# A product of ones behind the spreading product, and the cap of both w_out placed behind GpSimd's addition for block 1

## The chip, the core and the metric

The kernel runs on one core of a Trainium2 chip. The metric is the device time of one execution in microseconds (us); five executions of the kernel before gave a median of 307.3 us (306.88, 307.03, 307.30, 309.13 and 309.36). The core has TensorE (PE; PEld is its weight load), VectorE (DVE), ScalarE (ACT), GpSimd (POOL) and SyncE (SP), which here only issues transfers. Each engine takes its instructions in the order in which the program gives them.

## What is computed

A polynomial attention without a softmax, and behind it a gated feed-forward layer:

```python
# q, k, v: (4, 4, 1088, 32); S1, S2: (8, 32); w_gate, w_val: (128, 1536); w_out: (1536, 128)
a = einsum('rd,bhsd->bhsr', S1, x); b = einsum('rd,bhsd->bhsr', S2, x)      # phi(x): 8 x 8 = 64 features
q_p, k_p = phi(q), phi(k)
kv  = einsum('bhsf,bhsd->bhfd', k_p, v);  z = sum(k_p, axis=2)
x   = einsum('bhsf,bhfd->bhsd', q_p, kv) / (einsum('bhsf,bhf->bhs', q_p, z) + 1e-6)
x   = x.transpose(0, 2, 1, 3).reshape(4352, 128)
out = (1 / (1 + exp(-(x @ w_gate))) * (x @ w_val)) @ w_out
```

S1, S2 and the three weights arrive as 64-bit floats, seen as pairs of 32-bit words, and are narrowed to 32 bits inside the kernel.

## The kernel before, in words

**Tiling.** The feed-forward layer is cut into chunks of 512 tokens (`tok_chk`) and twelve blocks `j` of 128 hidden units. `w1` issues one "wave": the gate and value products of one block for one chunk into the two banks of a PSUM tile `wave` (pool `psm`, two buffers), then ScalarE's sigmoid; its `glu` is VectorE's product of the two. `w2` adds block `j` into the chunk's output sum (`moeout`). `slot(group, waves)` places a piece of attention work and then that many waves. A float32 product appears in the profile as two MATMUL instructions, so a wave is four (512 columns each), and a `w2` step two.

**The start.** The attention of batch 0 must give the first 512 columns of `xT`, the layer's input, before any wave can run. On TensorE the order is: products of ones (`warm`, L255 to L261, whose result nothing reads), the turning of S, `kps` (keys times S), `ab` (queries times S, L542), `gram` with its 36 small products (L468), two further `ab`, the spreading product `spread_z` (L497), the denominators `dps` (L730), the key-value sums `kvz` in two groups of 40 and 32 instructions (L638, called from `rest`), the transposition `ndps` (L708), the numerators `nps` (L749), one more `warm(256)` (L868), and then the waves (L363). Between these VectorE makes the outer products `kp` (L530), the mask `zm` and `zb` behind the spreading product (L508, L520), the transposition `dT` of the denominators (L741), and in `divide` (L757) a reciprocal and two halves of `xT` (L776), each behind a transposition `rb` (L765). ScalarE copies between: `kvd` (L674) and `nd` (L721).

**The narrowing.** `narrow` (L83) works in four steps, with a `yield` between them: step 0 is GpSimd's `cap` (L97) and ScalarE's `tail` (L101), which both read what the transfer brought; step 1 is VectorE's two instructions on `head` (L105, L109); step 2 is ScalarE's `square` (L117) and GpSimd's addition into `head` (L118); step 3 is VectorE's product into `w_sb` (L127). For blocks 0 and 1 `narrow_01(part, step)` (L187) takes three parts: part 0 is gate and value of block 0, part 1 gate and value of block 1, part 2 both w_out. For the other blocks it is `narrow_w(j, step)`, three weights of one block at a time. Steps 0 of all three parts stand ahead of `spread_z()` (L844). Steps 1 and 2 of part 0 stand in `rest` (L863), which `dn` runs between denominators and numerators. In `divide` the function `head1` (L870) is run between the first `rb` and the first half of `xT`; it has part 1's step 1, part 0's step 3, part 1's step 2, and step 0 of blocks 2 and 3. Part 1's step 3 and part 2's steps 1 and 2 follow behind `divide`; part 2's step 3 comes in the second wave (L374).

**Transfers.** All loads of the first batch are issued by SyncE (the keys by ScalarE) at the very start, in the order of L239 to L249. Nothing of them depends on the lines that the change touches.

Of the kernel before, what the change touches and what calls it, by code (L numbers as in the profile page):

```python
# [20 lines left out]
def kernel(  # L21
# [61 lines left out]
    def narrow(out, bits, eng, bank=None, copies=None):  # L83

        p, n, m = bits.shape[:3]
        lo, hi = bits[:, :, :, 0].bitcast(U32), bits[:, :, :, 1]

        def tmp(dt, tag, bufs):
            return sbN.tile([P, 3, P], dt, tag=tag, name=tag, bufs=bufs)[:p, :n, :m]

        cap, tail = tmp(I32, "cap", 6), tmp(I32, "tail", 5)
        eng.tensor_scalar(  # L97
            out=cap.bitcast(F32), in0=hi.bitcast(F32), scalar1=122880.0, scalar2=-122880.0,
            op0=ALU.min, op1=ALU.max,
        )  # L100
        nc.scalar.activation(out=tail, in_=lo, func=ACTF.Copy, scale=2.0**-29)  # L101
        yield

        head = tmp(I32, "head", 3)
        nc.vector.tensor_scalar(  # L105
            out=head, in0=cap, scalar1=3, scalar2=0x3FFFFFF8,
            op0=ALU.logical_shift_left, op1=ALU.bitwise_and,
        )
        nc.vector.scalar_tensor_tensor(  # L109
            out=head, in0=cap, scalar=-0x40000000, in1=head, op0=ALU.bitwise_and, op1=ALU.bitwise_or  # L110
        )
        yield
        square = cap.bitcast(F32)
        if bank:
            square = pso.tile([P, 512], F32, tag=bank, name="square")[:, : n * m]
            square = square.rearrange("p (n m) -> p n m", n=n)
        nc.scalar.activation(out=square, in_=cap.bitcast(F32), func=ACTF.Square)  # L117
        nc.gpsimd.tensor_tensor(out=head, in0=head, in1=tail, op=ALU.add)  # L118
        yield

        head = head.bitcast(F32)
        if copies:
            square, head = (
                bass.AP(tensor=x.tensor, offset=x.offset, ap=[list(x.ap[0]), [0, copies], [1, m]])
                for x in (square, head)
            )
        nc.vector.scalar_tensor_tensor(  # L127
            out=out, in0=square, scalar=1.265625 * 2.0**-30, in1=head, op0=ALU.is_ge, op1=MUL
        )
        yield  # L130
# [44 lines left out]
    def narrow_w(j, step):  # L175
        if not 0 <= j < NJ:
            return
        n, jj = divmod(j, 2)
        if wide:
            if step == 0:  # L180
                narrowing[j] = narrow(
                    w_sb[:, :, j, :], w_in[n][:, :, jj], nc.gpsimd, "acc1" if j < NJ - 2 else None
                )
            next(narrowing[j])


    def narrow_01(part, step):  # L187
        if wide:
            if step == 0:
                i = (slice(0, 2), part) if part < 2 else (2, slice(0, 2))  # L190
                narrowing["01", part] = narrow(
                    w_sb[:, i[0], i[1]],
                    w_in[0][:, i[0], i[1]],
                    nc.gpsimd,
                    "acc0" if part else "acc1",
                )
            next(narrowing["01", part])
# [57 lines left out]
    def warm(*cols):  # L255
        t = psm.tile([P, 2, 512], F32, tag="wave", name="warm")
        one = [bass.AP(tensor=ones.tensor, offset=ones.offset, ap=[list(ones.ap[0]), [0, n]]) for n in cols]
        x = bass.AP(tensor=ones.tensor, offset=ones.offset, ap=[list(ones.ap[0]), [0, P]])
        for r in one:
            n = r.shape[-1]  # L260
            nc.tensor.matmul(out=t[:, 0, :n], lhsT=x, rhs=r, start=True, stop=True)  # L261
# [265 lines left out]
    def outer(b, pi, j0=0, j1=NJK):  # L527
        a0 = KAB[b][:, pi, j0:j1]
        ap = [list(a0.ap[0]), [2 * R, 2 * (j1 - j0)]]
        nc.vector.tensor_tensor(  # L530
            out=KP[b][:, pi, j0:j1].rearrange("p j m (i l) -> p (j m) i l", i=R),
            in0=bass.AP(tensor=a0.tensor, offset=a0.offset, ap=ap + [[1, R], [0, R]]),
            in1=bass.AP(tensor=a0.tensor, offset=a0.offset + R, ap=ap + [[0, R], [1, R]]),
            op=MUL,
        )
# [6 lines left out]
    def ab(a_of=None, b_of=None, pool_b=None):  # L542

        mm = []
        if a_of is not None:
            aps = psm.tile([P, 2, 512], F32, tag="wave", name="aps")
            mm.append((a_of, aps, sa))
        if b_of is not None:
            pool, tag = (ps2, "two") if pool_b is None else pool_b
            bps = pool.tile([P, 2, 512], F32, tag=tag, name="bps")  # L550
            mm.append((b_of, bps, sb))
        for c in range(2):
            for m in range(2):
                for (bb, pr, n), dst, sx in mm:
                    h = 2 * pr + m
                    rows = slice(32 * h, 32 * h + 32)
                    t0, tn = q_chk[n]
                    nc.tensor.matmul(
                        out=dst[64 * c : 64 * c + 64, m, : 32 * tn],
                        lhsT=sx[rows, :],  # L560
                        rhs=qT_of[bb][rows, t0 : t0 + tn, c, :],
                        start=True,
                        stop=True,
                    )
        if a_of is not None:
            w = 32 * q_chk[a_of[2]][1]
            ASB[a_of] = sbA.tile([P, 2, 256], F32, tag="asb", name="asb", bufs=2)
            nc.scalar.copy(out=ASB[a_of][:, :, :w], in_=aps[:, :, :w])
        if b_of is not None:

            def mult():
                bb, pr, n = b_of
                if bb not in QP:
                    QP[bb] = sbA.tile([P, 2 * H * W1], F32, tag="qp", name="qp")
                t0, tn = q_chk[n]
                w = 32 * tn
                nc.vector.tensor_tensor(  # L577
                    out=half(QP[bb], n).rearrange("p (m c) w -> p c m w", m=2)[:, pr],
                    in0=bps[:, :, :w],
                    in1=ASB[b_of][:, :, :w],  # L580
                    op=MUL,
                )

            return mult
# [256 lines left out]
    spread_z, mask_z = gram()  # L841
    mult00 = ab(None, (0, 0, 0))
    mult10 = ab(None, (0, 1, 0), (psm, "wave"))
    for part in range(3):  # L844
        narrow_01(part, 0)
    spread_z()
    for pi in range(2):
        outer(0, pi, 0, 5)
    mult00()
# [20 lines left out]
    def head1():  # L870
        narrow_01(1, 1)
        narrow_01(0, 3)
        narrow_01(1, 2)
        narrow_w(2, 0)
        narrow_w(3, 0)

    divide((0, 4), (4, 8), between=head1)
    narrow_01(1, 3)
    narrow_01(2, 1)
# [86 lines left out]
```

## Time and profile before

The profiled execution took 307.03 us, of which 305.0 us lie between its first and last instruction (the span); 2.0 us lie around it.

| engine | busy us | share of the span | instructions |
|---|---|---|---|
| TensorE | 297.5 | 98% | 1364 |
| TensorE weight load | 138.3 | 45% | 1364 |
| VectorE | 155.3 | 51% | 267 |
| ScalarE | 80.7 | 26% | 150 |
| GpSimd | 35.4 | 12% | 63 |

Busy time is summed from the first to the last instruction of each engine's records; TensorE's products are pipelined, so that a busy TensorE need not be one at its peak. The profile also tells the share of full speed that TensorE's clock was granted (PEclk). In the chain of work that ended last, TensorE has 96% of the span, 58% of it in the waves and 30% in `moeout`. In a listing by time, a bracket such as `[1.18 <-DVE zb L520]` says how long the engine had been idle before the row and what ended that.

### The profile page before, as it was taken

How to read it: one execution, taken by the hardware profiler on the slowest of the kernel's cores; microseconds unless marked ns; L12 is line 12 of the kernel's file. 1: busy time of each engine (PE TensorE's matmuls, PEld its weight loads, DVE VectorE, ACT ScalarE, POOL GpSimd, SP SyncE). 2: the span in 40 equal slices, each digit the busy share in tenths (PEclk: the TensorE clock that was granted, in tenths of full speed). 3: DMA queues.
4: the chain of work that ended last, by engine and by line, in shares of the span. 5: the costliest groups of instructions: out<-in, count | busy, mean ns of one | idle time of the engine just before them, and what ended most of it. 6: DMA issues, size and time to landing. Idle time of an engine off the chain costs nothing.

```text
span 305.0 us, 3608 instructions
## 1 busy us (share of the span) xinstructions
PE 297.5 (98%) x1364; PEld 138.3 (45%) x1364; DVE 155.3 (51%) x267; ACT 80.7 (26%) x150; POOL 35.4 (12%) x63
## 2 busy tenths in 40 slices
PE   8799999999999999999999999999999999999994
PEld 3454434444344444443444444444444444444683
DVE  7887888865546544564365543645232223222331
ACT  3455542221123222212222222221222222222220
POOL 1545560410000500000004100000000000000000
PEclk9789999999999999999999999999999999999999
DMA  7992531597102594440004910200010000200011
GB/s 230 335 335 62 126 116 42 133 225 190 65 0 37 120 160 69 78 157 27 0 8 125 212 39 2 36 0 2 0 20 15 0 0 5 31 0 0 8 27 17
DMA packets 29585, 23.29 MB, mean 76 GB/s; under 512 B 20928, under 2 KB 24512, under 8 KB 29568
## 3 DMA queue, kind: packets, MB, share of 16 engines
q1 hardware_dynamic: 25200, 15.21, 18.5%
q0 software_dynamic: 3456, 7.09, 11.9%
q10 hardware_dynamic: 912, 0.77, 0.9%
q8 instruction: 10, 0.16, 0.2%
q14 instruction: 7, 0.06, 0.1%
HBM read 19.80 MB, written 3.26 MB: 76 GB/s over the span
## 4 chain that ended last, share of the span: by engine, by line
PE 96%; DVE 1%; DMA 1%; issue 0%; ACT 0%; SPq 0%; DVEq 0%
PE wave L363 58%; PE moeout L320 30%; PE nps L749 2%; PE dps L730 2%; PE kvz L652 1%; PE kps L451 1%; PE kvz L638 1%; DMA s_in<-in_S_dram 1%; PE cqps L597 1%; PE warm L261 0%; PE ndps L708 0%; DVE kT L428 0%; PE gram L474 0%; PE kvz L661 0%; DVE qp L577 0%
## 5 line engine op out<-in xcount | busy, mean ns | idle before, releaser
L363 PE MATMUL wave<-xT,w_sb 128*128 128x512 f32 (+1 forms) x436 | 192.0, 566 | 0.0
L384 DVE TENSOR_TENSOR g<-wave,sg 128x512 f32<-128x512 f32 x102 | 70.4, 690 | 132.8 <-ACT sg L371 132.5
L363 PEld LDWEIGHTS wave<-xT,w_sb 128*128 128x128 f32 x436 | 83.3, 191 | 93.1 <-issue 88.7
L371 ACT ACTIVATE sg<-wave 128x512 f32<-128x512 f32 x102 | 60.9, 597 | 201.9 <-PE wave L363 201.9
L320 PE MATMUL moeout<-g,w_sb 128*128 128x512 f32 (+1 forms) x216 | 105.4, 576 | 0.0
L320 PEld LDWEIGHTS moeout<-g,w_sb 128*128 128x128 f32 x216 | 39.5, 190 | 43.6 <-issue 38.2
L621 POOL DMA_DIRECT2D qp<-dq x12 | 7.0, 587 | 109.5 <-DMA dq<-cq 109.5
L118 POOL TENSOR_TENSOR head<-head,tail 128x384 int32<-128x384 int32 (+2 forms) x14 | 13.6, 971 | 17.9 <-DVE head L109 14.3
L530 DVE TENSOR_TENSOR kp<-kab 128x1152 f32<-128x1152 f32 (+2 forms) x10 | 10.8, 1096 | 0.0
L630 DVE TENSOR_TENSOR qp<-qp,bq 128x1152 f32<-128x1152 f32 (+1 forms) x7 | 9.1, 1294 | 0.3 <-DMA bq<-dq 0.2
L109 DVE SCALAR_TENSOR_TENSOR head<-cap,head 128x384 int32<-128x384 int32 (+2 forms) x14 | 7.5, 535 | 0.5
L330 DVE STREAM_TRANSPOSE o_sb<-moeout 128x512 f32<-128x512 f32 (+1 forms) x9 | 6.1, 680 | 2.6 <-PE moeout L320 2.5
L97 POOL TENSOR_SCALAR cap<-w_in 128x384 f32<-128x384 f32 (+1 forms) x13 | 7.0, 543 | 1.3 <-DMA w_in<-in_moe_w_out_dram 1.3
L101 ACT ACTIVATE tail<-w_in 128x384 int32<-128x384 uint32 (+1 forms) x13 | 6.6, 524 | 2.0 <-DMA w_in<-in_moe_w_out_dram 2.0
L621 POOL DMA_DIRECT2D bq<-dq x12 | 6.9, 576 | 0.5 <-DMA out_dram<-o_sb 0.2
L776 DVE TENSOR_TENSOR xT<-nps,rb 128x576 f32<-128x576 f32 (+2 forms) x9 | 5.9, 661 | 1.9 <-PE nps L749 1.3
L127 DVE SCALAR_TENSOR_TENSOR w_sb<-square,head 128x384 f32<-128x384 f32 (+1 forms) x11 | 5.6, 519 | 1.9 <-POOL head L118 1.6
L730 PE MATMUL dps<-qp,zb 128*32 128x256 f32 (+1 forms) x64 | 5.4, 409 | 1.2 <-DVE zb L520 1.2
L261 PE MATMUL warm<-ones 128*128 128x512 f32 (+2 forms) x10 | 5.5, 682 | 1.0 <-DVE hm L267 1.0
L749 PE MATMUL nps<-qp,nd 64*32 64x256 f32 (+1 forms) x128 | 6.0, 432 | 0.4 <-ACT nd L721 0.4
L765 DVE STREAM_TRANSPOSE rb<-rc 128x576 f32<-128x576 f32 (+2 forms) x9 | 6.1, 680 | 0.3
L439 DVE STREAM_TRANSPOSE qT<-kq 128x512 f32<-128x512 f32 (+1 forms) x8 | 5.7, 715 | 0.0
(73 smaller groups left out, 85.2 us busy)
## 6 DMA issues: line engine op xcount, KB each, us to landing
qp<-dq POOLq DMA_DIRECT2D x12, 288.0 KB, 7.7
bq<-dq POOLq DMA_DIRECT2D x12, 288.0 KB, 8.6
v<-in_v_dram SPq DMA_DIRECT2D x16, 144.0 KB, 5.4
kq<-in_k_dram SPq DMA_DIRECT2D x3, 544.0 KB, 4.1
kq<-in_q_dram SPq DMA_DIRECT2D x3, 544.0 KB, 5.2
w_in<-in_moe_w_gate_dram SPq DMA_DIRECT2D x6, 256.0 KB, 5.6
w_in<-in_moe_w_val_dram SPq DMA_DIRECT2D x6, 256.0 KB, 5.4
w_in<-in_moe_w_out_dram SPq DMA_DIRECT2D x6, 256.0 KB, 7.2
```

Source lines behind the costliest of these rows:

```text
L97: eng.tensor_scalar(out=cap.bitcast(F32), in0=hi.bitcast(F32), scalar1=122880.0, scalar2=-122880.0, op0=ALU.min, op1=ALU.max,)
L109: nc.vector.scalar_tensor_tensor(out=head, in0=cap, scalar=-0x40000000, in1=head, op0=ALU.bitwise_and, op1=ALU.bitwise_or)
L118: nc.gpsimd.tensor_tensor(out=head, in0=head, in1=tail, op=ALU.add)
L320: nc.tensor.matmul(out=moe["acc"][:, :tw], lhsT=w_sb[:, 2, j, :], rhs=g[:, jj, :tw], start=(j == 0), stop=(j == NJ - 1),)
L363: nc.tensor.matmul(out=wv[:, which, jj * tw + o : jj * tw + o + tp], lhsT=w_sb[:, which, j0 + jj, :], rhs=xT[:, t0 + o : t0 + o + tp], sta ...
L371: nc.scalar.activation(out=sg, in_=wv[:, 0], func=ACTF.Sigmoid)
L384: nc.vector.tensor_tensor(out=g, in0=wv[:, 1], in1=sg, op=MUL)
L530: nc.vector.tensor_tensor(out=KP[b][:, pi, j0:j1].rearrange("p j m (i l) -> p (j m) i l", i=R), in0=bass.AP(tensor=a0.tensor, offset=a0.of ...
L621: get.dma_start(out=t[64 * c : 64 * c + 64, n * H * W1 : (n + 1) * H * W1], in_=bass.AP(tensor=d0.tensor, offset=d0.offset, ap=rows + [[1, ...
L630: nc.vector.tensor_tensor(out=q0, in0=q0, in1=half(BQ[b], n), op=MUL)
L730: nc.tensor.matmul(out=dps[32 * h : 32 * h + 32, :w], lhsT=zb[b % 2][:, h, :], rhs=half(QP[b], n)[:, 2 * (h % 2) + h // 2, :], start=True, ...
L749: nc.tensor.matmul(out=t[32 * h : 32 * h + 32, c, :w], lhsT=ND[b][rows, 32 * h : 32 * h + 32], rhs=half(QP[b], n)[rows, 2 * (h % 2) + h // ...
```

## The change

`narrow_01(2, 0)`, that is GpSimd's `cap` and ScalarE's `tail` of both w_out (128 x 256 elements each), moves from ahead of `spread_z()` into `head1`, behind part 1's step 2, where GpSimd's addition for block 1 is issued. And behind `spread_z()` stands `warm(512)`: a product of the array of ones with itself, 128 x 128 by 512 columns, into a PSUM tile of tag `wave`. Nothing else changes; no transfer moves.

```diff
@@ -841,9 +841,10 @@
     spread_z, mask_z = gram()
     mult00 = ab(None, (0, 0, 0))
     mult10 = ab(None, (0, 1, 0), (psm, "wave"))
-    for part in range(3):
+    for part in range(2):
         narrow_01(part, 0)
     spread_z()
+    warm(512)
     for pi in range(2):
         outer(0, pi, 0, 5)
     mult00()
@@ -871,6 +872,7 @@
         narrow_01(1, 1)
         narrow_01(0, 3)
         narrow_01(1, 2)
+        narrow_01(2, 0)
         narrow_w(2, 0)
         narrow_w(3, 0)
```

## The prediction, made before the changed kernel was run

> **What bounds the kernel now.** I read three views. First the page's row of the granted clock over 40 slices of 7.6 us, and its chain of the work that ended last:
>
> ```profile
> PEclk9789999999999999999999999999999999999999
> ...
> PE 96%; DVE 1%; DMA 1%; issue 0%; ACT 0%; SPq 0%; DVEq 0%
> ```
>
> TensorE is the end of everything, and it has full clock except in the second and third slice. (The first 4 us are also shown as full, but the six `warm` instructions there take 3.79 us, twice what their 2,304 columns take later at 0.43 us per 512.) So what is won at the start stays won, if no other engine is late behind it; what happens on another engine counts only where TensorE waits.
>
> Then busy time by windows, cut where the clock changes (start and end in us, then length, busy time of each engine with its instructions, granted clock, DMA share, GB/s):
>
> ```profile
> 4.18:7.59 3.41, 3.06 (x57) 1.47 (x56) 3.15 (x8) 0.96 (x4) 0.45 (x2) 1.00 1.01 290
> 7.59:11.01 3.42, 1.90 (x48) 1.19 (x48) 3.39 (x8) 1.45 (x6) 1.29 (x3) 1.00 1.08 282
> 11.01:14.42 3.41, 3.02 (x80) 2.13 (x69) 3.15 (x10) 1.28 (x4) 1.76 (x3) 0.50 1.07 376
> 14.42:17.84 3.42, 3.06 (x22) 1.84 (x22) 2.08 (x7) 1.81 (x5) 1.58 (x3) 0.50 1.07 372
> 17.84:21.25 3.41, 3.38 (x12) 1.92 (x11) 3.02 (x6) 1.87 (x5) 2.23 (x3) 1.00 1.06 355
> ```
>
> The clock is halved from 11.01 to 17.84 us, 6.83 us, which I cut into two equal windows. The window before the fall is the one in which TensorE did least: 1.90 of 3.42 us.
>
> Third, the chain of waits in order of time (start, us, what), with a stretch of the second batch at full clock for comparison:
>
> ```profile
> 10.24 0.23 DVE zb L520
> 10.47 0.14 issue
> 10.60 0.74 PE dps L730 x8
> 11.34 2.27 PE kvz L638 x72
> 13.62 0.02 issue
> 13.64 0.28 ACT kvd L674
> 13.91 0.04 issue
> 13.96 0.49 PE ndps L708
> 14.45 0.02 issue
> 14.47 0.28 ACT nd L721
> 14.74 0.04 issue
> 14.79 1.11 PE nps L749 x16
> 15.89 1.15 PE warm L261 x2
> 17.04 3.90 PE wave L363 x12
> 20.94 0.03 issue
> 20.97 1.12 PE moeout L320 x2
> ...
> 66.05 1.28 PE kvz L652 x72
> ```
>
> The same 72 instructions take 2.27 us at half and 1.28 us at full clock. From 10.60 us on, nearly everything on the path is TensorE at half speed.
>
> **The product of ones.** It removes nothing and adds two MATMULs of 512 columns with their weight loads. Later, four such instructions of a wave take 1.72 us in the chain, 0.43 each: 0.86 us at full clock. In the listing of TensorE the spreading product starts at 9.01 and takes 0.41, and `dps` is issued at 10.60 after 1.18 us idle, released by VectorE's `zb`. So the product runs from about 9.42 to 10.28, inside that gap: cost nothing. The cover is VectorE's `qp`, `zm` and `zb`; were the clock half there, 1.72 us would overrun the gap by 0.54 us. Its PSUM buffer was last read by ScalarE's `asb`, done at 8.24: no wait. It shifts the rotation of the two `wave` buffers by one; the next user, `warm(256)`, then gets the buffer that VectorE's `qp` finished reading at 10.07, long before it is due.
>
> What it can bring is the clock. It lifts the window 7.59 to 11.01 from 1.90 to 2.76 us busy, 81%. The trace gives both ends: 3.06 us (90%) kept full clock in the window before, 1.90 us (56%) lost it. Busy time flatters small products, so I also counted columns streamed: `bps`, the spreading product and three quarters of `dps` come to about 0.85 us of array time (25%), with the product 1.7 us (50%); the window that kept its clock held about 1.8 us (53%; rest of `warm`, `kps`, `aps`, `gram` at 64 or 32 rows in parallel). By either count the new window lies much nearer to the one that kept the clock. I take it that the clock stays.
>
> A rule speaks against this. The Trainium skill, "TensorE: Matmul & The Clock Gate" (section on why this matters for your kernels) asks for no idle gap over some 3 us and lets the clock fall after an idle window. The longest gap here was 1.18 us, far below, and yet the row shows the fall at 11.01. By the rule filling the gap has no effect (gain 0, the fall has another cause); by the row a window of 56% already falls, and filling it is worth what follows. The row decides, with the rule kept as a rival. The same page's Part 1 says that the window lasts 3413 ns, which the 6.83 us here (twice that) agree with, and that it runs free of the kernel's start. No view of one execution can show the latter, but five times in two groups (306.9 to 307.3 and 309.1 to 309.4) would fit it: in another phase the product falls into another window.
>
> **If the clock stays full from 11.01.** Durations at full clock are taken from the second batch's rows. `dps` 0.57 (at 73.14) ends at 11.17; `kvz` 1.28 ends at 12.45 (its last outer product is ready at 11.65, in time); `kvd` 12.75; `ndps` (two took 0.22 there; I take 0.25) 13.04; `nd` 13.34; `nps` 0.6 ends at 14.0, against 15.89. `warm(256)` ends at 14.45. So TensorE is 1.9 us earlier, but now VectorE is late: from 11.57 to 14.14 it has no idle time (`dT`, two heads, reciprocal, `rb`), then part 0's product L127, which waited 0.16 us for ScalarE's `square` behind `kvd` and now need not. So the first half of `xT` starts at 14.55 instead of 15.99: 1.44 us. The first wave can start at 15.0 (was 17.04), needs 8 x 0.215 = 1.72 us, the second as much: TensorE is done with both at 18.44 instead of 20.94. Next is `moeout` for block 0, which needs part 2's L127. That stands at the end of VectorE's list:
>
> ```profile
> 15.99 0.42 DVE L776 TENSOR_TENSOR xT<-nps,rb 128x256 f32<-128x256 f32 x1 [1.27 <-PE nps L749]
> ...
> 19.89 0.69 DVE L384 TENSOR_TENSOR g<-wave,sg 128x512 f32<-128x512 f32 x1 [0.36 <-ACT sg L371]
> 20.50 0.88 DVE L127 SCALAR_TENSOR_TENSOR w_sb<-square,head 128x256 f32<-128x256 f32 x2
> ```
>
> From 15.99 to about 20.94 (the first of the last row's two) are 4.95 us, 0.36 of them waiting for the sigmoid, which will now be early. So 14.55 + 4.59 = 19.15, and `moeout` starts at 19.2 against 20.97: **1.77 us earlier**, TensorE waiting 0.75 us for VectorE. After this TensorE had no idle time before, and the third wave's weights (L127 of block 2, about 19.9) come ahead of its 20.1. The gain stays to the end: the transfers for blocks 2 to 5 show no wait when their caps ran, and later ones are issued at the start and due over 15 us after.
>
> **The moved cap and tail.** Moved are one GpSimd instruction (0.90 us, at 11.04, while VectorE worked; 0.39 alone at 8.95) and one on ScalarE (0.44 us); no transfer, and SyncE's queue is not touched. Both waited for w_out's landing at about 10.99. Neither was on the path: GpSimd idled 0.87 us before its next addition, ScalarE 0.68 us before `rc`. Gain where they leave: nothing, up to the delay if w_out lands later in another run (then `rc` and `kvd` stand behind it in ScalarE's queue). Where they arrive, GpSimd's caps of blocks 2 and 3 (1.02 us from 14.98) start 0.4 to 0.55 later and end by 16.6; queued behind is part 2's addition, due at 14.55 + 2.24 + 0.16 = 16.95. ScalarE's three tails end at about 16.6, so `square` of part 2, possible at 16.3, starts 0.3 later and ends at 17.0, and the first sigmoid at 17.6: both ahead of VectorE, which comes to the gate product at 18.1. VectorE's heads for part 2 want the cap at 16.05; it is there at 15.5. Cost nothing; bounds 0 and +0.4 us, the latter from VectorE beside GpSimd (a head took 0.46 beside the addition at 13.22 against 0.25; another 1.01 against 0.56). I take 0.1.
>
> Sum, against this execution: 307.03 - 1.77 + 0.1 = 305.36, so **305.4 us**, 0.6% below the median of 307.3. About 0.5% is what a measurement of this kernel tells from no change.
>
> **The rivals.** *The fall stays at 11.01* (the threshold is above 81% busy, or the skill's rule holds): the product is hidden, the path unchanged: 307.1. For it: 90% is the only row that kept the clock. *The fall comes one window later and lasts one*: the window 11.01 to 14.42 at full clock would hold only some 2.7 us busy. `xT` is early, but the waves run at half from 15.0 to 17.84 (1.42 of 1.72 done), so both end at 19.86 and `moeout` starts 1.1 us early: 305.9. *The fall comes at 14.42 and the window behind does not lift it*: slower. Before, 3.06 us busy lifted the clock and 3.02 did not; the changed window 14.42 to 17.84 would hold 2.84, waiting for `xT` till 15.0. At half until 21.25, the first wave ends at 18.44, the second at 21.57: 0.6 us later than before, 307.6; a third such window costs half of 3.41 more, 309.3, which is also where the upper group of the five times lies. Its place is the waves, where TensorE alone is the path; it decides once the half clock reaches beyond about 20 us. That the product runs at half clock in its gap (+0.54) belongs to this case.
>
> **How the numbers follow.** Full clock throughout 0.55; fall at 11.01 as before 0.14; one window later 0.08; waves at half clock 0.23. The last reaches beyond 308.8 in most of its chance, since the phase of the window would then change the median's group too. Faster by over 0.5%: 0.50 + 0.02; within: 0.05 + 0.14 + 0.06 + 0.04; slower: 0.19. The range runs from 304.7 (TensorE's whole 2.4 us) to 307.9. The likeliest case alone: 304.7 to 305.9.
>
> **What would show it.** Right: PEclk 1.00 from 4 to 300 us, `kvz` near 1.3 us, the first half of `xT` at 14.5, `moeout` at 19.2 released by L127. Wrong: half clock anywhere from 11 us on, or `dps` later than 10.6.

## The result, and the profile after

The changed kernel takes 305.72 us in the median of 43 executions (305.39 to 311.1); the kernel before, 80 executions beside it, 307.18 (304.99 to 313.74). The ratio is 0.997, with a 95% interval of [0.9956, 0.9983]. It leaves out executions more than 1.5% above the fastest of their kernel, nine of the 80 and one of the 43, so it shows less than the medians do (305.72 / 307.18 = 0.995). The profiled execution took 305.45 us, 303.7 of them the span, against 307.03 and 305.0. Faster, then, and by the ratio within the 0.5% that counts as no change.

The page's row of the granted clock, and the head of the chain that ended last:

```profile
PEclk9999999999999999999999999999999999999999
...
PE 94%; DVE 2%; DMA 1%; issue 1%; ACT 0%; SPq 0%; DVEq 0%; ACTq 0%
```

The two slices with half clock in them are gone, and VectorE's share of the path has gone from 1% to 2% (about 6 us). Where, the chain in order of time shows (start, us, what):

```profile
10.52 0.23 DVE zb L520
10.76 0.14 issue
10.89 0.64 PE dps L730 x8
11.53 1.32 PE kvz L638 x72
...
14.34 0.42 DVE w_sb L127
14.76 0.33 DVE xT L776
15.09 0.36 DVE rb L765
15.45 0.02 issue
15.47 0.03 DVE xT L776
15.51 0.31 issue
15.82 0.41 DVE w_sb L127
16.23 0.60 DVE head L105
16.83 0.02 issue
16.85 0.42 DVE head L109
17.28 0.28 DVE head L105
17.56 0.02 issue
17.58 0.66 DVE head L109
18.24 0.27 issue
18.52 0.68 DVE g L384
19.20 0.34 DVE w_sb L127
19.54 0.04 issue
19.58 1.12 PE moeout L320 x2
```

`kvz` takes 1.32 us instead of 2.27: full clock. From 14.34 to 19.54 the path is VectorE's list, and `moeout` of block 0 ends it. The two executions don't start alike (`dps` at 10.89 here, 10.60 before, mostly because S landed 0.23 later), so the distance from `dps` to `moeout` is the measure used from here on: 8.69 us, before 10.37. In TensorE's list the row of `moeout` says what it waited for:

```profile
19.58 1.12 PE L320 MATMUL moeout<-g,w_sb 128*128 128x512 f32 x2 [0.73 <-DVE w_sb L127]
```

Busy time in the same two stretches as before, in the same columns:

```profile
7.59:11.01 3.42, 2.84 (x60) 1.46 (x62) 3.39 (x8) 1.70 (x5) 1.31 (x3) 1.00 1.09 283
11.01:14.42 3.41, 2.67 (x97) 1.54 (x93) 3.31 (x10) 1.64 (x6) 0.73 (x1) 1.00 1.06 373
```

2.84 us busy where there were 1.90. But these stretches are cut at the edges that the clock's windows had in the profile of before. In the traces of all runs, the time between two changes of the clock is a whole multiple of 3.413 us (2 of them in the fall of before, 84 to 88 elsewhere), and the record of the clock begins with the change to full clock at the start, which gives the edges of each profiled execution. Before, it begins at 4.19 us, here at 5.78: the clock's own windows here were 5.78 to 9.19 and 9.19 to 12.61, with 3.16 and 3.07 us busy. So this one profile does not yet show that it was the product that kept the clock.

One row of VectorE's list is out of line, part 2's first head with 0.67 us (start, us, engine, line, operation; first before, then after), and GpSimd's row beside it suggests why:

```profile
17.48 0.28 DVE L105 TENSOR_SCALAR head<-cap 128x256 int32<-128x256 int32 x1
```

```profile
15.82 0.41 DVE L127 SCALAR_TENSOR_TENSOR w_sb<-square,head 128x256 f32<-128x256 f32 x1
16.15 0.67 DVE L105 TENSOR_SCALAR head<-cap 128x256 int32<-128x256 int32 x1
```

```profile
15.27 1.40 POOL L97 TENSOR_SCALAR cap<-w_in 128x256 f32<-128x256 f32 x3
```

The caps, the moved one first, last until 16.67, half a microsecond into that head, which ends at 16.82.

### The profile page after: what moved, and what is told of

Read it like the earlier page. It is cut to its first block, busy times and chain, and to the rows that moved or that the text cites. A ratio compares the mean times of both kernels' runs of the same rounds, so it can differ in the third digit from the quotient of the medians.

```text
span 303.7 us, 3614 instructions
## 1 busy us (share of the span) xinstructions
PE 296.7 (98%) x1366; PEld 137.0 (45%) x1366; DVE 155.1 (51%) x267; ACT 80.8 (27%) x150; POOL 34.7 (11%) x63
## 4 chain that ended last, share of the span: by engine, by line
PE 94%; DVE 2%; DMA 1%; issue 1%; ACT 0%; SPq 0%; DVEq 0%; ACTq 0%
PE wave L363 57%; PE moeout L320 30%; PE dps L730 2%; PE nps L749 1%; PE kvz L652 1%; PE kps L451 1%; DMA s_in<-in_S_dram 1%; PE cqps L597 1%; PE kvz L638 0%; DVE head L109 0%; DVE w_sb L127 0%; DVE head L105 0%; PE ndps L708 0%; PE gram L474 0%; PE kvz L661 0%
## 5 line engine op out<-in xcount | busy, mean ns | idle before, releaser
L127 DVE SCALAR_TENSOR_TENSOR w_sb<-square,head 128x384 f32<-128x384 f32 (+1 forms) x11 | 5.7, 519 | 3.8 <-POOL head L118 3.8
L261 PE MATMUL warm<-ones 128*128 128x512 f32 (+2 forms) x12 | 6.6, 680 | 1.0 <-DVE hm L267 1.0
L117 ACT ACTIVATE square<-cap 128x384 f32<-128x384 f32 (+1 forms) x11 | 5.1, 463 | 1.8 <-DVE w_sb L127 1.7
```

## The experiments

Every execution lists its mean granted clock. One window of half clock costs 3.41 x 0.5 / 305 = 0.0056 of it, and the values do lie in steps of that size, so that below 0.9955 at least one window was at half. In the three series of the kernel before, on three chips, they sort like this:

| executions of the kernel before (178) | number | median us |
|---|---|---|
| no window at half | 49 | 305.80 (fastest 305.05) |
| one (clock near 0.994) | 16 | 306.62 |
| two (0.986 to 0.9905) | 57 | 307.49 |
| between one and two (0.9905 to 0.9935) | 13 | 307.86 |
| three or more | 14 | 310.07 |
| clock read as 0.9955 to 1.000, yet 308.4 us or more | 29 | 309.61 |

So the kernel before loses the clock in 100 of 178 executions, and in 28% of them it does not and is as fast as the changed one. The profile of before is one of the commonest group. Three theories stood at the start: **1**, the product keeps the clock and is the whole gain, and the moved cap costs something through contention; **2**, the moved cap is needed; **3**, the product decides nothing and the clock's windows fall as they fall.

**The two parts alone, and both again.**

```diff
# e1_product_only, e7_product_only_again
     spread_z()
+    warm(512)
# e2_cap_only
-    for part in range(3):
+    for part in range(2):
         narrow_01(part, 0)
...
         narrow_01(1, 2)
+        narrow_01(2, 0)
```

> The product of ones alone; the cap of both w_out stays where it was. Theory 1 (the product keeps the clock and is the whole gain; the moved cap costs some 0.35 us because VectorE's first head of part 2 then runs beside GpSimd's caps, 0.67 us against 0.28): no half clock between 4 and 300 us, that head back at 0.25 to 0.30 us, `moeout` of block 0 starting 8.3 us after `dps` (both parts: 8.69; before: 10.37), time 305.0 to 305.4, at least 0.3 us below both parts together. Theory 2 (the moved cap is needed, since a late w_out would hold ScalarE and GpSimd up): no faster than both parts, 305.7 or more, with more runs above 307. Theory 3 (the product decides nothing, the fall of the clock is a matter of the window's phase alone): times spread from 305 to 308 like the kernel before, median near 307.

> The moved cap alone, without the product of ones. Theory 1: the clock falls near 11 us for 6.8 us in most executions as before, time 307.0 to 307.6, not below the kernel before; in executions without a fall not below 305.3, where the kernel before reaches 305.0. Theory 2: faster than the kernel before by 0.3 us or more, and fewer runs above 307.6. Theory 3: as before, with the same spread.

> Both parts, the changed kernel itself, beside the single parts on the same chip. Theory 1: 305.4 to 305.8, narrow, above the product alone by 0.3 to 0.4. Theory 2: at or below the product alone. Theory 3: spread from 305.4 to 308.

The product alone: 305.47 us (9 executions, none below 0.9955), ratio to before 0.9945 [0.992, 0.997]; its median is 0.19 below that of both parts, not the 0.3 that theory 1 expected at least. The moved cap alone: 307.68 (22, of which 15 below), ratio 1.0002 [0.9974, 1.003]. Both: 305.66 (10, none below), 0.9961 [0.9939, 0.9983]. Theory 2 falls: the cap alone brings nothing, and the product alone all of it. Theory 3 describes the kernel before, where chance decides whether the clock falls, but not the kernel with the product, where it stays.

The profiled execution of the cap alone was one without a fall, and so shows what the product does to the path itself. TensorE's row of `dps` there, with no product in the gap, and the chain's end:

```profile
10.89 0.64 PE L730 MATMUL dps<-qp,zb 128*32 128x256 f32 x8 [1.18 <-DVE zb L520]
```

```profile
19.20 0.34 DVE w_sb L127
19.58 1.13 PE moeout L320 x2
```

Again 8.69 us, the distance with both parts. In these two profiles, both at full clock, the one with the product and the one without take the same time to the hundredth: the product is worth nothing but the clock, and in its gap it costs nothing. The edges lay nearly alike in the two (the record begins at 5.89 with the cap alone), and here the window of 9.30 to 12.72 kept the clock without the product, with 2.24 us busy: the changed kernel's profile might have kept it without the product, too.

Like with like is the product alone, whose record begins at 4.02 (before: 4.19). The window that holds the gap, in the columns of the windows above:

```profile
7.43:10.85 3.42, 2.84 (x60) 1.42 (x61) 3.39 (x8) 1.80 (x5) 1.28 (x3) 1.00 1.10 243
```

2.84 us busy, and the clock stayed, where 1.90 lost it before. Its second run and that of both parts beside it begin at 3.91 and 3.79, hold 2.98 and 3.08 us in that window, and kept the clock as well. The profile of the product alone has `dps` at 10.81 and

```profile
16.07 0.30 DVE L105 TENSOR_SCALAR head<-cap 128x256 int32<-128x256 int32 x1
```

```profile
19.14 1.12 PE L320 MATMUL moeout<-g,w_sb 128*128 128x512 f32 x2 [0.35 <-DVE w_sb L127]
```

8.33 us: 0.36 less than with both parts; the head alone is 0.37 shorter.

> The product of ones alone, once more, to measure its distance from both parts with more runs (first time: 305.47 against 305.66 median, fastest 305.06 against 305.33). Theory 1: median 305.0 to 305.5, fastest 305.0 to 305.1, no run below a mean clock of 0.995. Rival (the distance was chance): fastest at 305.3 or above, median 305.6 or more.

305.75 us (16, 305.10 to 307.59), none below 0.9955. The fastest is as theory 1 had it, the median as the rival had it: the spread of late transfers is wider than the distance looked for. Its profile shows one: `kvz` waited 0.51 us for v. Over both runs the product alone has 305.51 in 25 executions, both parts 305.72 in 76 (with the 44 the first comparison lists): a difference of 0.21 whose interval, by resampling, reaches from 0.41 below to 0.12 above. The trace shows it, the medians don't.

**Contention, or a late cap?** Both parts, with step 0 of block 3 placed later:

```diff
# e6_both_block3_later, e11_block3_later_again, against both parts
         narrow_w(2, 0)
-        narrow_w(3, 0)
...
     narrow_01(2, 2)
+    narrow_w(3, 0)
```

> Both parts, but step 0 of block 3 (GpSimd's cap, ScalarE's tail) goes from head1 to behind step 2 of part 2, so that GpSimd is done with its caps about 0.5 us before VectorE comes to part 2's first head. Theory contention (the moved cap costs time because that head runs beside the caps): the head falls from 0.67 to about 0.3 us and `moeout` starts 0.3 to 0.45 us earlier after `dps` (8.69 to about 8.3); fastest run 305.0 to 305.1. Rival theory lateness (the head waits for its own cap, which now comes later): the cap of part 2 keeps its place, so the head stays at 0.6 to 0.7 and the time at 305.4 to 305.7.

The moved cap keeps its place; only a neighbour leaves. VectorE's head and GpSimd's caps in its profile:

```profile
16.23 0.28 DVE L105 TENSOR_SCALAR head<-cap 128x256 int32<-128x256 int32 x1
```

```profile
15.35 0.91 POOL L97 TENSOR_SCALAR cap<-w_in 128x256 f32<-128x256 f32 x2
```

The caps end at 16.26, the head takes 0.28, and `moeout` at 19.28 is 8.30 us behind `dps` at 10.98. So the head did not wait for its own cap; it was slow beside the others. One of ScalarE's tails moved along with block 3's cap, but with both parts these end at 15.54, before the head starts, and can't be what held it up. Time: 305.52 (22, fastest 304.99), ratio to before 0.9954 [0.993, 0.9978]. Once more, on one chip with both parts:

> Both parts once more, beside the version with block 3's cap placed later, on one chip. Theory contention: 305.4 fastest, median 305.6 to 305.8, above that version by 0.2 to 0.4. Rival: no difference above 0.1.

> Both parts with step 0 of block 3 behind step 2 of part 2, once more. Theory contention: fastest 305.0 to 305.1, median 305.2 to 305.5. Rival: as both parts, 305.4 fastest.

Both parts 305.76 (22, fastest 305.34; head 0.68), block 3 later 305.39 (22, fastest 305.18, a tenth above what was expected; head 0.28). The medians of the pair differ by 0.37, with an interval by resampling from -0.72 to +0.33. In the lower quartiles of all executions, which late transfers touch less, the product alone (305.28) and block 3 later (305.29) lie beside 305.50 for both parts (differences -0.22 with an interval from -0.42 to 0.00, and -0.21 from -0.31 to -0.14). This version is the best one measured with all of the change in it; the product alone is its equal.

**How much product?**

```diff
# e3_product_256: half        e4_product_1024: double
+    warm(256)                +    warm(512, 512)
# e5_thin: as long, a sixteenth of the array (the view of ones that is streamed is written short)
+    tt = psm.tile([P, 2, 512], F32, tag="wave", name="thin")
+    nc.tensor.matmul(out=tt[:32, 0, :], lhsT=ones[:32, :], rhs=ones_32x512, start=True, stop=True)
```

> The product at half the columns (256), the cap where it was. It lifts the busy time of the window in which the clock fell from 1.90 to about 2.33 of 3.41 us (68%), between the 56% that lost the clock and the 81% that kept it; by streamed columns 38% between 25% and 50%. Theory 1 with a threshold in busy time near 60%: as the product alone, 305.0 to 305.4. Theory 1 with a threshold above 70% (or 40% by columns): falls like before in most executions, median 306.5 to 307.3. Theory 3: no difference from before.

305.77 us; 4 of 22 below 0.9955. Between the two expectations: half the product keeps the clock in most executions, not in all. Where the windows' edges fall differs between executions, and with it how much of the gap one window holds; so no threshold in busy time can be read from these counts. In the profiles' first 24 us the emptiest windows that kept the clock have 2.23 us (both parts, 10.62 to 14.03) and 2.24 (the cap alone), 65% and 66%; the one that lost it has 56%.

> The product twice (two of 512 columns), the cap where it was. 1.72 us in a gap of 1.2: `dps` starts about 0.5 us later than with one product (11.3 to 11.4 instead of 10.8), TensorE then is late for the first half of `xT` by some 0.4 us. Theory 1: clock never falls, time 305.4 to 305.9. Rival (more work on TensorE is free here, or steadies the clock further): 305.0 to 305.4.

305.90 us (fastest 305.52), none of 22 below. As theory 1 had it; TensorE's rows show the overrun, with no idle time ahead of `dps`:

```profile
9.71 1.97 PE L261 MATMUL warm<-ones 128*128 128x512 f32 x4
11.61 0.64 PE L730 MATMUL dps<-qp,zb 128*32 128x256 f32 x8
```

> In place of the product a thin one of the same length: ones of 32 rows and 32 columns, 512 columns streamed, so one sixteenth of the array for the same 0.86 us; the cap where it was. If what the clock's windows count is busy time: like the product alone, under one run in ten with a mean clock below 0.995, median 305.0 to 305.5. If they count how much of the array works: falls as often as before (27 of 50 runs below 0.995), median 306.5 to 307.9.

305.72 us; 7 of 22 below 0.9955. The thin product's row has 1.04 us, the full one's 1.11. Neither expectation: fewer falls than without a product (100 of 178), more than with the full one of the same length (none in 25). So how much of the array works seems to count beside the time; 22 executions don't give the weight, and this stays open (the next runs have one more sign of it).

**The executions above 308.4 us at full reported clock.**

```diff
# e8_no_first_ones: the kernel before; e9_no_first_ones_product: with the product
-    warm(512, 512, 128)
```

> The kernel before without the first three products of ones (512, 512 and 128 columns at L265). It asks what the executions of the kernel before are that take 308.5 to 312 us at a mean clock of 0.999 or 1.000 (13 of 69 in the second series). Theory late lift: in them the clock was never lifted at the start, and the record of the clock, which begins with its first change, shows nothing of it. Then here, where TensorE does little in its first 5 us, most executions take 308.5 to 311, `kps` to `kvz` take twice their time, and the mean clock still reads near 1.0. Rival (those executions are slow for late transfers): leaving the products out changes little, median within 0.5 us of the kernel before.

> The same without the first three products of ones, with the product of ones behind the spreading product, cap where it was. Theory late lift: at half clock that product takes 1.7 us and delays `dps` by about 0.5, but it fills the window, so the clock is lifted one or two windows sooner: 307 to 308.5, below the run without it by 1 us or more. Rival: within 0.3 us of it, or slower by the 0.5 us.

Without the first ones 310.16 us (5 executions, 309.46 to 313.12; the profiled one reports a mean clock of 1.000); with the product 308.26 (21, 306.32 to 310.57). TensorE's rows, first of before, then without the first ones, then without them and with the product:

```profile
5.75 0.72 PE L451 MATMUL kps<-kT,sk 64*32 64x288 f32 x16
```

```profile
6.28 1.21 PE L450 MATMUL kps<-kT,sk 64*32 64x288 f32 x16
...
13.65 2.49 PE L637 MATMUL kvz<-kp,v 128*32 128x64 f32 x72
```

```profile
6.03 1.21 PE L450 MATMUL kps<-kT,sk 64*32 64x288 f32 x16
...
13.00 1.06 PE L729 MATMUL dps<-qp,zb 128*32 128x256 f32 x8
13.86 1.48 PE L637 MATMUL kvz<-kp,v 128*32 128x64 f32 x72
```

`kps` takes 1.21 us against 0.72 before, and `kvz` 2.49 without the product, though the clock row says 1.00 throughout: until its first change the record reads as full. With the product `kvz` takes 1.48, while without it the first twelve wave instructions still took 5.10 us against 3.71. The records say the same: they begin at 13.90 us with the product and at 22.42 without. The two windows ahead of 13.90, both still at half clock:

```profile
7.07:10.48 3.41, 3.41 (x76) 1.63 (x68) 2.29 (x4) 1.94 (x5) 0.57 (x2) 1.00 1.09 254
10.48:13.90 3.42, 3.42 (x24) 1.37 (x20) 2.84 (x6) 0.44 (x2) 0.84 (x3) 1.00 1.06 376
```

TensorE is busy throughout in both. The first, all of products on a part of the array (32 to 128 rows by 32 or 64 columns), did not lift the clock; the second, with 2.05 us of the full product, did. This points the same way as the thin product. A clock not lifted at the start thus gives times like those of the 29 executions in the last line of the table. None of these 29 was itself profiled; that they are such executions is an inference. With the product, executions of that kind are faster: 19 of the 21 without the first ones take 307.28 to 308.82. With both parts, 8 of 76 executions lie there, at 307.71 to 308.73 with the clock read as 1.00, and the next below is at 307.22. If these are the counterpart of the 29, the product does not prevent a late lift (8 of 76 against 29 of 178) but shortens it. None of the eight was profiled.

## Why the prediction was right, and where its sum was off

**The main step held.** Filling the gap keeps the clock: 100 of 178 executions below 0.9955 before, 1 of 76 with both parts, 0 of 25 with the product alone. Weighing busy time and streamed columns against the two neighbouring windows gave the right side: in the profile of the product alone, with its edges nearly where they lay before, the window has 2.84 us (2.76 was worked out) and keeps the clock. Against the rule of a 3 us gap, which the prediction kept as a rival, the row was right: a gap of 1.18 us goes with a lost clock when the window around it is 56% busy, and filling it keeps the clock.

**What comes late next** was named rightly: not TensorE but VectorE's list, ending in part 2's L127. TensorE waits 0.73 us there (0.75 was worked out). From `dps` to `moeout` the working had 19.2 - 10.6 = 8.6 us; the product alone has 8.33. So the term of 1.77 us was too small: the product alone gives 10.37 - 8.33 = 2.04. Of the missing 0.27, 0.16 lie ahead of the first half of `xT`, which starts 3.79 us behind `dps` (14.60 - 10.81) and not 3.95: the working added two durations of VectorE in full, where each next row starts about 0.08 before the end of the last.

**The mis-sized term** is the moved cap, taken as 0.1 us with a bound of +0.4 "from VectorE beside GpSimd": it is 0.36 to 0.39 (8.69 against 8.33 and 8.30), the upper bound. The working had even placed the end of the caps (16.6) behind the head's start (16.05), and asked only whether the head's own cap was ready. The two errors nearly cancel: 2.04 - 0.36 = 1.68 against the 1.67 of the sum. That 305.4 lies within 0.05 us of the profiled execution is therefore luck in part. (Its later start, 0.29, is made up for by less time around the span, 1.76 against 2.05; 0.1 us is lost behind `moeout`.)

**The common base was wrong in one way.** The sum was made against one execution with a two-window fall, as if every execution had it. 28% of them have none and gain nothing (they lose what the moved cap costs, 0.36 in the traces), while the 14 of 178 with three or more windows at half lie 4.35 us above the changed kernel's median (310.07 against 305.72). The 29 in the last row may gain only about 1.7, from 309.61 to the 307.9 around which the eight lie. The median gained 1.46 us where the sum had 1.67. That the phase of the windows would spread the gain was written down as a doubt, with five times for evidence, and not carried into the forecast.

**The rivals.** The fall one window later, and the waves at half clock, happened in none of the profiles of the changed kernel; at most the one execution of 76 at 311.1 us (mean clock 0.981) is of the last kind. The fall at 11.01 as before did not happen either. `dps` came at 10.89, later than the 10.6 that was named as a sign of being wrong; but so it did with the cap alone, where no product stands in the gap, and the delay comes from the first 6 us (`kps` starts at 6.04 and 6.03 in these two, before at 5.75). That SyncE's and GpSimd's queues lose nothing by the removed wait for w_out held as far as the times can tell: the cap alone is at 1.0002, with an interval of 0.3% to either side.

## What to carry to other kernels

When TensorE's clock halves, look at how busy the window before the fall was and not only at the longest gap; a product of ones in the gap, no longer than the gap, cost nothing here and kept the clock. Where the windows' edges lie in a profile belongs to the reading: a profile in which the clock stays may have its edges elsewhere. Compare executions by their mean granted clock before trusting one profile: such a fall may be a matter of chance, and the gain is then a share of executions. When work is moved to an idle stretch of GpSimd, check what VectorE does there, not only whether the result is ready in time.

## What the runs showed of the hardware

- The clock's record reads as full until its first change. In the run without the first ones it says 1.00 where `kps` takes 1.21 us for 0.72; durations show a halved clock that the row doesn't.
- The granted clock changes at whole multiples of 3.413 us from its last change (2, 84, 86, 87 and 88 of them in the traces), and the first change came anywhere between 3.79 and 6.24 us in the profiles with the first ones.
- VectorE's head on 128 x 256 integers takes 0.28 us alone, 0.46 beside GpSimd's addition and 0.67 beside its caps; in both cases it ends 0.15 us behind GpSimd's row (13.97 against 13.82, 16.82 against 16.67), which looks as if it were held up until GpSimd is done; no run here tells that from being slowed.
- With a thin product (32 x 32 of the array) of the same length the clock is lost in 7 of 22 executions, with the full one in none of 25. And a window busy throughout with products on parts of the array (3.41 of 3.41 us) did not lift a halved clock, while the next, with a full product in it, did.
- With the clock kept, executions still spread by over 1 us with the landing of the first loads: in one profile of both parts `kvz` waited 0.94 us for v, and `moeout` came at 20.54.
